# A fused attention and FFN kernel on one core: transposes of head pairs give way to x's, statistics are released after the second block-product group, and kept products run on ScalarE or VectorE

## The chip, the core and the metric

One core of a Trainium2 chip runs the whole program. Its engines are TensorE (PE in the profile; PEld is its weight load), VectorE (DVE), ScalarE (ACT), GpSimd (POOL) and SyncE (SP, which only issues DMAs). ScalarE and GpSimd issue DMAs too. Each engine works through its own instructions strictly in order; what is still waiting at the head of a queue holds up everything behind it. The metric is the device time of the program in microseconds, as the median of several runs.

## The reference

```python
# q, k, v: 8 batches, 12 heads, 448 positions, 64 wide
scores = scale * np.matmul(q, k.transpose(0, 1, 3, 2))
attn = np.maximum(scores, 0.0) ** 2 / S
attn_out = np.matmul(attn, v)
x = attn_out.transpose(0, 2, 1, 3).reshape(B, S, H * D)      # 8 x 448 x 768
mu, var = mean and variance of x over its 768 columns
xn = (x - mu) / np.sqrt(var + 1e-06) * g_ln
ch = np.maximum(xn @ w_ch1, 0.0) @ w_ch2                     # 768 -> 3072 -> 768
return x + ch
```

The output is float32. The kernel computes in bfloat16 with float32 sums. It leaves the division by the standard deviation to the end: the factor `rstd` of a row passes through the ReLU and is applied when the second FFN product is evacuated.

## The kernel before, in words

**Stages.** The eight batches `b` follow each other. While the FFN of one batch runs on TensorE, the attention of the next is slipped in between in "visits". Attention works on three pairs of head groups per batch, numbered `n` = 3b to 3b+2 (`NPER` = 3). A pair's q and k come in by GpSimd DMAs into one staging tile (`load_pair`, L423), are turned by one SyncE DMA transpose (L429) into one of two slots (`RING` = 2), and are used by seven score products (`att_QK`, L610). Each score tile is scaled and clipped by ScalarE (L619) or VectorE (L621) and squared by VectorE (L634) or, rarely, by GpSimd (L636). `att_AV` (L676) multiplies by v into a PSUM tile, which is copied in two parts to `xT_all` (L385 on ScalarE, L387 on VectorE): 2x384 columns and 2x64 columns. GpSimd sums these parts for the mean (L767 to L770). `after_x` turns x back with SyncE DMA transposes into `x_all` (L797), takes batch statistics from there on VectorE (`bn_stats` L822 and L825, `bn_aggr` L828), the root on ScalarE (L838) and the reciprocal on VectorE (L840). The result is `rstd`.

**First FFN product.** `ffn_1` (L971) and `ffn_1_slot` (L989) make one 128-row tile of hidden units with six matmuls. For batches 3 to 6, three groups (`G_STEADY` = 3) of four tiles are instead made with seven block products, P1 to P7, instead of eight (`ffn_1_product`, L1193; a Strassen-like scheme). In each group the two PSUM banks are reused, so three intermediate results are copied out and kept: c1 after P1, c2 after P6, p5 after P5 (`keep`, L1225). `add_relu` (L1219) adds a kept result to a bank and applies ReLU on VectorE: C11 after P2, C22 after P7, C12 after P3. C21 is a plain ReLU after P4 (L1234). The group's three banks of work depend on each other: P6 needs c1 out, P5 needs C11 out, P7 needs c2 out, P3 needs p5 out, P4 needs C22 out. The kept tiles lie in `o_all`, whose two rows also carry finished output to the store DMAs, so a keep waits for the last store of that row (`o_done`).

**Second FFN product.** `ffn_w` (L1428) does the same with pairs of 128-row output tiles, again in seven products; its evacuations (L1436) multiply by `rstd` and add x. `ffn_2` (L1519, evacuated by L1535) is the plain form. `store_tile` (L1557) sends the results out from ScalarE's and SyncE's queues. L1384 and L1066 to L1070 are VectorE's block sums for the two schemes.

**What sets the order.** Nothing runs by the order of the source. `Order` is a planner: each piece of work is an `Op` with candidate engines, a cost in ns for each, dependencies, and a `key` (lower goes first among equals). `best` takes the op that can start first by the planner's clock, and for an op with several engines the engine that would finish it first; `commit` emits the instruction then and there and advances that engine's clock. `segment` chooses at each step between the FFN's next product and the next attention visit by the same clock. So a dependency or a cost that is written into the planner changes in which order, and on which engine, everything afterwards is emitted; the waits that the hardware sees come from the data alone. `later(...)` is a dependency on something not yet planned and `now_known` fills it in. `stats_gate` is such a dependency: for batches 3 to 6 the statistics (keyed 4.0 down to 3.8, after almost everything) may be planned only once `"seven past"` is filled in, which happens when the last of the three groups is through. In `commit`, a DMA on SyncE occupies that engine's clock for 0.55 of its modelled transfer.

Of the kernel before, what the change touches and what calls it, by code (L numbers as in the profile page):

```python
# [41 lines left out]
class Order:  # L42
# [39 lines left out]
    def commit(self, op, eng, t0):  # L82
        cost = op.cost[op.engs.index(eng)] if isinstance(op.cost, tuple) else op.cost
        if op.load is not None and eng != "POOL":
            t0 = max(t0, self.lanes[-8])
        op.t0 = t0
        self.free[eng] = t0 + cost - (self.OVER[eng] if op.load is None else 0.0)
        if op.port and eng in self.port:
            self.port[eng] = t0 + cost - (140.0 if eng == "POOL" else 0.0)
        if op.load is not None and eng == "POOL":  # L90
            total, each = op.load
            start = max(self.dma_free, t0 + cost + 1300.0)
            self.dma_free = start + total
            self.loads.append((start, self.dma_free, each))
            op.t1 = self.dma_free + 700.0
        elif op.load is not None:
            left, each = op.load
            start = t = max(self.ring[eng], t0 + cost + 1300.0)
            while left > 0:
                edge, wait = None, 0.0  # L100
                for a, z, e in self.loads:
                    if a <= t < z:
                        edge, wait = z, e
                    elif t < a and (edge is None or a < edge) and not wait:
                        edge = a
                rate = 16.0 / (each + wait)
                span = left / rate if edge is None else min(left / rate, edge - t)
                left -= rate * span
                t += span
                if left < 1e-6:  # L110
                    break
            self.ring[eng] = t
            self.lanes.append(t + 900.0)
            if eng == "SP":
                self.free["SP"] = t0 + max(cost, 0.55 * (t - start))
            op.t1 = t + 900.0 + (0.2 * (t - start) if eng == "SP" else 0.0)
        else:
            op.t1 = t0 + cost + self.LAT[eng]
        op.emit(eng)
        self.log.append((t0, cost, eng, op))  # L120
# [82 lines left out]
def kernel(  # L203
# [10 lines left out]
    nc = tc.nc  # L214
# [3 lines left out]
    Act = mybir.ActivationFunctionType  # L218
# [195 lines left out]
    def load_pair(n):  # L414

        b, pn = divmod(n, NPER)
        free = [ops["qk_free", 0]] if n == 2 * NPER else [later("turn", n - 1)]
        ld = []
        for t, src in enumerate((q, k)):
            for half in range(2):  # L420
                def emit(eng, t=t, src=src, half=half):
                    h0 = half * 6 + 2 * pn
                    nc.gpsimd.dma_start(  # L423
                        qk_stage()[half * T:(half + 1) * T, t].rearrange("p j (h d) -> p j h d", d=D),
                        src[b, h0:h0 + 2].rearrange("h (p j) d -> p j h d", j=J))
                ld.append(load(dma_ns(2 * S, 256), emit, free, 900.0))

        def turn(eng):
            nc.sync.dma_start_transpose(qk_slot(n).rearrange("p t j c -> p (t j) c"),  # L429
                                        qk_stage().rearrange("p t j c -> p (t j c)"))  # L430
        free = [later("qk_end", n - RING)] if n >= 2 * NPER + RING else []
        ops["turn", n] = R.add("SP", 100.0, turn, ld + free, key=0.0, load=(2 * J * P, 18.0))
        now_known(ops["turn", n], "turn", n)
        ld = []
        free = [later("av_end", n - RING)] if n >= 2 * NPER + RING else [later("av_done", 1)]
        for half in range(2):
            def emit(eng, half=half):
                if "v" not in homes:
                    v_t = v_pool.tile([P, H // 2 * S], bf16, tag="v1")
                    homes["v"] = v_t  # L440
                h0 = half * 6 + 2 * pn
                nc.gpsimd.dma_start(  # L442
                    v_slot(n)[half * T:(half + 1) * T],
                    v[b, h0:h0 + 2].rearrange("h (p j) d -> p h (j d)", j=J))
            ld.append(load(dma_ns(2 * T, 1792), emit, free, 700.0))
        ops["v_ld", n] = ld
# [213 lines left out]
    def att_AV(n, s):  # L660
# [28 lines left out]
        if b == 0:  # L689
            for half in range(2):  # L690
                def evac(eng, half=half):
                    ki = pn + half * NPER
                    copy(eng, xT_of(b)[:, ki, :], av_st[n][half])
                ev = R.add(("DVE", "ACT"), (620.0, 560.0), evac, [op], key=-1.0)
                f_use(ev)
                evs.append(ev)
        else:
            def evac(eng, cols, o):
                i = av_st[n, 1][:, :, cols]
                if len(o.shape) == 4:  # L700
                    o, i = o.rearrange("p m h c -> p h m c"), i.rearrange("p h (m c) -> p h m c", c=P)
                copy(eng, o, i)
            if b == 1:
                parts = [(slice(0, S), xT_of(b)[:, pn::NPER, :])]
            else:
                t, t_left = xT_of(b)
                parts = [(reg(b), t[:, :, pn::NPER, :]), (left(b), t_left[:, pn::NPER, :])]
            for cols, o in parts:
                w = cols.stop - cols.start
                evs.append(R.add(("DVE", "ACT"), (160.0 + 2.08 * w, 150.0 + 1.7 * w),  # L710
                                 lambda eng, cols=cols, o=o: evac(eng, cols, o), [op] + free, key=-1.0))
            slot_use(evs)
        ops["x", n] = evs
        if n == NPER - 1:
            for ev in held_relu:
# [401 lines left out]
    W_OF = {"P1": ("A", 0, 0), "P2": ("A", 0, 1), "P6": "S2", "P5": "S1", "P7": "S3", "P3": "S4", "P4": ("A", 1, 1)}  # L1117
    X_OF = {"P1": "B11", "P2": "B21", "P6": "T2", "P5": "T1", "P7": "T3", "P3": "B22", "P4": "T4"}

    FLIGHT = 4  # L1120
    AWAY = 1700.0

# [47 lines left out]
    def ffn_1_product(b, g, name):  # L1170
# [51 lines left out]

        def keep(key):
            def emit(eng):
                nc.scalar.copy(kept(key), e["ps", bank])  # L1225
            free = [later("av_done", b)] if b == LAST_B else o_done[e["o"] if key == "c2" else 1 - e["o"]]
            e[key] = R.add("ACT", 560.0, emit, [op, *free], key=-3.0)
        if name in ("P1", "P6", "P5"):
            keep({"P1": "c1", "P6": "c2", "P5": "p5"}[name])
        elif name != "P4":  # L1230
            add_relu(*{"P2": ("C11", 0, 0, "c1"), "P7": ("C22", 1, 1, "p5"), "P3": ("C12", 0, 1, "c2")}[name])
        else:
            def relu(eng):
                nc.scalar.activation(h_out(1, 0), e["ps", "x"], Act.Relu)  # L1234
            e["C21"] = R.add("ACT", 560.0, relu, [op], key=-3.0)
            if b < LAST_B:
                f_banks[:] = [e["C12"], e["C21"]]
                f_tags.reverse()
# [3 lines left out]
            h_done(b, range(4 * g, 4 * g + 4), [e[c] for c in ("C11", "C12", "C21", "C22")], op)  # L1242
            if b < LAST_B and g == G_STEADY - 1:
                now_known(op, "x sums used", b)
                now_known(e["C12"], "seven past", b, 5)
                now_known(e["C21"], "seven past", b, 15)

# [615 lines left out]
```

## Time and profile before

| what | value |
|---|---|
| median of 3 runs | 527.24 us (527.17 to 527.32) |
| the profiled execution's own time | 527.36 us |
| its span, first to last instruction | 525.6 us |
| granted TensorE clock | 1.000 |
| TensorE busy | 503.0 us, 4416 matmuls |
| VectorE busy | 390.8 us, 738 instructions |
| ScalarE busy | 236.9 us, 373 instructions |
| GpSimd busy | 170.4 us, 201 instructions |
| score ReLU on ScalarE, L619 | 127 x 927 ns |
| score ReLU on VectorE, L621 | 32 x 1087 ns |
| squares on VectorE, L634 | 158 x 720 ns |
| x's DMA transposes, L797 | 21, median 8.0 us from issue to landing |
| pairs' DMA transposes, L429 | 18, median 4.4 us from issue to landing |
| keeps in `o_all` on ScalarE, L1225 | 36 x 535 ns |

The span is what the instructions fill; the run's own time is 1.76 us longer. In the listing of a timeline, a line has its start and length in us, the engine, the source line, output and input tiles, the shape and the number of merged instructions; a bracket at the end tells how long the engine stood idle before it and which instruction ended that wait. Busy time adds the records of an engine; a sum over windows shows where an engine is idle.

### The profile page before, as it was taken

To read this page: it belongs to the slowest core of one execution; us is meant where nothing else is said; L and a number is where in the kernel's file an instruction comes from. 1 tells how busy PE (TensorE), PEld (TensorE's weight loads), DVE (VectorE), ACT (ScalarE), POOL (GpSimd) and SP (SyncE) were. 2 spreads that over 40 slices of the span, in tenths; PEclk is the share of its full clock that TensorE was granted. 3 is DMA by queue.
4 is the path that set the end of the run, shared out by engine and by line. 5 is a ranking of instruction groups with operands and counts; after the bars stand their busy time and mean duration, and the time that the engine had idled before them with its cause. 6 is when DMAs were issued, how large, how long until landed. Compare 5 with 4: busy or idle time off the path is not lost.

```text
span 525.6 us, 10787 instructions
## 1 busy us (share of the span) xinstructions
PE 503.0 (96%) x4416; PEld 305.8 (58%) x4416; DVE 390.8 (74%) x738; ACT 236.9 (45%) x373; POOL 170.4 (32%) x201
## 2 busy tenths in 40 slices
PE   4899999999999999999899999999999999999997
PEld 3444455455564445567456675566655666569864
DVE  5988648946887878855988479756789578976853
ACT  5977612523214654255622676145722466125300
POOL 7420501434542545451650455323633022200000
PEclk9999999999999999999999999999999999999999
DMA  9999999889777848892992976966883610123022
GB/s 190 197 186 195 199 193 127 80 107 137 82 143 81 80 64 102 106 152 36 90 109 54 126 77 81 114 110 56 89 99 65 126 19 2 30 58 64 2 62 60
DMA packets 145949, 51.89 MB, mean 99 GB/s; under 512 B 123238, under 2 KB 144108, under 8 KB 145900
## 3 DMA queue, kind: packets, MB, share of 16 engines
q0 software_dynamic: 82224, 25.50, 45.8%
q1 hardware_dynamic: 59036, 18.82, 20.8%
q10 hardware_dynamic: 4640, 6.88, 4.6%
q8 instruction: 34, 0.56, 0.4%
q14 instruction: 15, 0.12, 0.1%
HBM read 51.91 MB, written 11.01 MB: 120 GB/s over the span
## 4 chain that ended last, share of the span: by engine, by line
PE 76%; DVE 10%; DMA 4%; ACT 4%; issue 3%; POOL 2%; SPq 0%; ACTq 0%; DVEq 0%; POOLq 0%
PE f_ps L1428 20%; PE f_ps L971 16%; PE f_ps L1519 12%; PE f_ps L1193 8%; PE ps L989 5%; PE sc L610 5%; PE ps L676 4%; DVE at_all L634 4%; PE x_ps L1193 2%; DMA out_dram<-o_all 2%; ACT at_all L619 2%; PE y_ps L1193 2%; ACT xT_all L385 1%; DMA x_all<-xT_all 1%; DMA f<-in_k_dram 1%
## 5 line engine op out<-in xcount | busy, mean ns | idle before, releaser
L619 ACT ACTIVATE at_all<-sc 128x896 bf16<-128x896 f32 x127 | 110.6, 927 | 74.0 <-PE sc L610 67.9
L634 DVE TENSOR_TENSOR at_all<-at_all 128x896 bf16<-128x896 bf16 x158 | 110.0, 720 | 1.3 <-ACT at_all L619 1.2
L1428 PEld LDWEIGHTS <-h 128*128 128x128 bf16 x708 | 68.5, 98 | 50.5 <-issue 6.3
L971 PE MATMUL f_ps<-a,w 128*128 128x448 bf16 x474 | 93.6, 353 | 0.2 <-DVE h L1002 0.2
L423 POOL DMA_DIRECT2D t<-in_q_dram x36 | 41.9, 1314 | 133.8 <-DMA t<-t 112.6
L971 PEld LDWEIGHTS <-w 128*128 128x128 bf16 x474 | 44.9, 98 | 45.3 <-issue 5.8
L1428 PE MATMUL f_ps<-w,h 128*128 128x384 bf16 x360 | 62.8, 326 | 1.6 <-DVE o_all L1436 1.0
L442 POOL DMA_DIRECT2D v_t<-in_v_dram x36 | 27.2, 820 | 93.3 <-PE sc L610 66.5
L423 POOL DMA_DIRECT2D t<-in_k_dram x36 | 55.0, 2083 | 0.0
L610 PE MATMUL sc<-t 64*64 64x448 bf16 x672 | 49.3, 364 | 3.8 <-ACT at_all L619 2.0
L621 DVE TENSOR_SCALAR at_all<-sc 128x896 bf16<-128x896 f32 x32 | 34.8, 1087 | 22.8 <-PE ps L676 18.6
L1000 ACT ACTIVATE h<-f_ps 128x448 bf16<-128x448 f32 (+1 forms) x59 | 29.3, 497 | 43.8 <-PE f_ps L971 42.2
L989 PE MATMUL ps<-a,w 128*128 128x448 bf16 x228 | 48.3, 352 | 0.8 <-DVE xT_all L387 0.8
L1193 PEld LDWEIGHTS <-w 128*128 128x128 bf16 x432 | 40.7, 98 | 8.9 <-issue 6.7
L1219 DVE CUSTOM_DVE_ANT_0 h<-f_ps,o_all 128x448 bf16<-128x448 f32 x36 | 21.8, 618 | 29.0 <-ACT h L1000 21.2
L1519 PE MATMUL f_ps<-w,h 128*128 128x384 bf16 x240 | 40.2, 326 | 0.0
L610 PEld LDWEIGHTS <-t 64*64 64x64 bf16 x672 | 18.3, 106 | 26.7 <-issue 18.6
L1193 PEld LDWEIGHTS <-t 128*128 128x128 bf16 x318 | 30.3, 98 | 5.6 <-issue 2.3
L769 POOL TENSOR_TENSOR sum_t<-sum_t,xT_all 128x384 f32<-128x384 f32 (+2 forms) x25 | 23.4, 935 | 31.1 <-ACT xT_all L385 30.8
L1519 PEld LDWEIGHTS <-h 128*128 128x128 bf16 x240 | 23.2, 98 | 16.5 <-issue 1.4
L989 PEld LDWEIGHTS <-w 128*128 128x128 bf16 x228 | 22.2, 98 | 15.9 <-issue 0.9
L1000 ACT ACTIVATE h<-ps 128x448 bf16<-128x448 f32 x39 | 20.8, 545 | 21.9 <-PE ps L989 21.6
(152 smaller groups left out, 720.1 us busy)
## 6 DMA issues: line engine op xcount, KB each, us to landing
w<-in_moe_w_ch_dram POOLq DMA_DIRECT2D x4, 1152.0 KB, 38.5
out_dram<-o_all ACTq DMA_DIRECT2D x43, 96.0 KB, 2.4
t<-in_q_dram POOLq DMA_DIRECT2D x36, 112.0 KB, 4.3
t<-in_k_dram POOLq DMA_DIRECT2D x36, 112.0 KB, 5.2
v_t<-in_v_dram POOLq DMA_DIRECT2D x36, 112.0 KB, 3.4
out_dram<-o_all SPq DMA_DIRECT2D x35, 96.0 KB, 2.1
w<-in_moe_w_ch_dram POOLq DMA_DIRECT2D x4, 768.0 KB, 20.0
out_dram<-o_all ACTq DMA_DIRECT2D x13, 192.0 KB, 3.9
```

Of the source, the lines that this page charges most:

```text
L423: nc.gpsimd.dma_start(qk_stage()[half * T:(half + 1) * T, t].rearrange("p j (h d) -> p j h d", d=D), src[b, h0:h0 + 2].rearrange("h (p j) ...
L442: nc.gpsimd.dma_start(v_slot(n)[half * T:(half + 1) * T], v[b, h0:h0 + 2].rearrange("h (p j) d -> p h (j d)", j=J))
L610: nc.tensor.matmul(sc[rows_of(half), r, :S], turned[rows_of(r), 1, s, rows_of(half)], turned[rows_of(r), 0, :, rows_of(half)], start=True, ...
L619: nc.scalar.activation(attn[n, s], st[0][:, :, :S], Act.Relu, scale=rc2)
L621: nc.vector.tensor_scalar(attn[n, s], st[0][:, :, :S], rc2, 0.0, op0=Alu.mult, op1=Alu.max)
L634: nc.vector.tensor_mul(attn[n, s], attn[n, s], attn[n, s])
L971: nc.tensor.matmul(st[0], w1[:, ki, ni * P:(ni + 1) * P], xc[b][:, ki, :], start=(i == 0), stop=(i == K1 - 1))
L989: nc.tensor.matmul(st[0], w1[:, ki, ni * P:(ni + 1) * P], xc[b][:, ki, :], start=ki == 0, stop=ki == K1 - 1)
L1000: nc.scalar.activation(o, st[0][:, c], Act.Relu)
L1193: nc.tensor.matmul(e["ps", bank][:, n, :], a[:, k, n * P:(n + 1) * P], x[:, k, :], start=name in ("P1", "P2", "P5") and n == 0 and k == 0, ...
L1428: nc.tensor.matmul(e["ps", bank], a(k), w(k), start=new and k == 0, stop=k == KH - 1, skip_group_check=True)
L1519: nc.tensor.matmul(o_st["ps"], stat(u, m, ki), w2[:, ki, j * hd:(j + 1) * hd], start=(ki == 0), stop=(ki == K2 - 1))
```

## The change

Six edits. In the planner, a SyncE DMA whose descriptor cost is under 20 (the DMA transposes, which carry 18.0) occupies SyncE's clock for 1.3 instead of 0.55 of its modelled transfer. A pair's transpose may be planned only after the whole AV product of the pair two before it, and not merely after that pair's score products. The second part of an AV evacuation is planned after the first, and the PSUM slot is free after the last part. A kept product and the ReLU after P4 may go to ScalarE (560) or VectorE (620). The statistics' two gates are filled in after the second of three groups. No matmul is added or removed.

```diff
             if eng == "SP":
-                self.free["SP"] = t0 + max(cost, 0.55 * (t - start))
+                self.free["SP"] = t0 + max(cost, (1.3 if op.load[1] < 20.0 else 0.55) * (t - start))
...
-        free = [later("qk_end", n - RING)] if n >= 2 * NPER + RING else []
+        free = [later("qk_end", n - RING), later("av_end", n - RING)] if n >= 2 * NPER + RING else []
         ops["turn", n] = R.add("SP", 100.0, turn, ld + free, key=0.0, load=(2 * J * P, 18.0))
...
                 evs.append(R.add(("DVE", "ACT"), (160.0 + 2.08 * w, 150.0 + 1.7 * w),
-                                 lambda eng, cols=cols, o=o: evac(eng, cols, o), [op] + free, key=-1.0))
-            slot_use(evs)
+                                 lambda eng, cols=cols, o=o: evac(eng, cols, o), [op] + free + evs, key=-1.0))
+            slot_use(evs[-1])
...
+    EITHER = (("ACT", "DVE"), (560.0, 620.0))
...
         def keep(key):
             def emit(eng):
-                nc.scalar.copy(kept(key), e["ps", bank])
+                copy(eng, kept(key), e["ps", bank])
             free = [later("av_done", b)] if b == LAST_B else o_done[e["o"] if key == "c2" else 1 - e["o"]]
-            e[key] = R.add("ACT", 560.0, emit, [op, *free], key=-3.0)
+            e[key] = R.add(*EITHER, emit, [op, *free], key=-3.0)
...
             def relu(eng):
-                nc.scalar.activation(h_out(1, 0), e["ps", "x"], Act.Relu)
-            e["C21"] = R.add("ACT", 560.0, relu, [op], key=-3.0)
+                if eng == "ACT":
+                    nc.scalar.activation(h_out(1, 0), e["ps", "x"], Act.Relu)
+                else:
+                    nc.vector.tensor_scalar(h_out(1, 0), e["ps", "x"], 0.0, None, op0=Alu.max)
+            e["C21"] = R.add(*EITHER, relu, [op], key=-3.0)
...
             if b < LAST_B and g == G_STEADY - 1:
                 now_known(op, "x sums used", b)
+            if b < LAST_B and g == 1:
                 now_known(e["C12"], "seven past", b, 5)
                 now_known(e["C21"], "seven past", b, 15)
```

## The prediction, made before the changed kernel was run

> **What bounds the kernel now.** I read the page's busy times first, then the windows, then TensorE's timeline for every wait, then the other engines around the longest ones.
>
> ```profile
> PE 503.0 (96%) x4416; PEld 305.8 (58%) x4416; DVE 390.8 (74%) x738; ACT 236.9 (45%) x373; POOL 170.4 (32%) x201
> PEclk9999999999999999999999999999999999999999
> ```
>
> ```profile
> 30.00:180.00 150.00, 150.00 (x1220) 78.92 (x1219) 110.67 (x226) 66.30 (x108) 50.54 (x55) 1.00 0.96 134
> 180.00:462.00 282.00, 272.69 (x2307) 168.38 (x2305) 218.59 (x392) 134.44 (x210) 104.04 (x121) 1.00 0.65 82
> ```
>
> TensorE bounds it, at full clock. From 30 to 180 us its records leave no idle time; from 180 to 462 us, where batches 3 to 6 run, they leave 282.00 - 272.69 = 9.3 us. The matmuls are not touched, so an order that removed every wait there would gain 9.3 us. That caps the change. These are the longer waits:
>
> ```profile
> 195.24 0.97 PE L1428 MATMUL f_ps<-w,h 128*128 128x384 bf16 x5 [0.57 <-DVE h L1002]
> 234.11 1.30 PE L989 MATMUL ps<-a,w 128*128 128x448 bf16 x6 [0.77 <-DVE xT_all L387]
> 260.54 0.32 PE L1428 MATMUL f_ps<-v_t,x_all 128*128 128x384 bf16 x1 [1.15 <-DVE o_all L1436]
> 295.00 0.73 PE L1193 MATMUL f_ps<-t,w 128*128 128x224 bf16 x6 [0.52 <-ACT o_all L1225]
> 331.62 1.14 PE L1428 MATMUL f_ps<-v_t,h 128*128 128x384 bf16 x6 [0.48 <-DVE o_all L1436]
> 365.53 0.73 PE L1193 MATMUL f_ps<-v_t,w 128*128 128x224 bf16 x6 [1.11 <-DVE h L1219]
> 385.63 0.32 PE L1428 MATMUL f_ps<-v_t,x_all 128*128 128x384 bf16 x1 [1.20 <-DVE o_all L1436]
> 428.45 0.74 PE L1193 MATMUL f_ps<-x_all,t 128*128 128x224 bf16 x6 [0.71 <-DVE h L1219]
> 458.31 2.11 PE L1428 MATMUL f_ps<-w,h 128*128 128x384 bf16 x12 [0.99 <-DVE o_all L1436]
> ```
>
> They add to 7.50 us; the other 1.8 us are waits under 0.25 us. Nearly all were ended by VectorE. Around 260 us it did this:
>
> ```profile
> 254.30 1.00 DVE L822 BATCH_NORM_STATS2 st<-x_all 128x6 f32<-128x384 bf16 x2
> 255.23 0.99 DVE L825 BATCH_NORM_STATS2 st<-x_all 128x6 f32<-128x384 bf16 x2
> 259.27 0.17 DVE L840 RECIPROCAL r_t<-r_t 128x4 f32<-128x4 f32 x1
> 259.87 0.61 DVE L1436 SCALAR_TENSOR_TENSOR o_all<-f_ps,r_t,x_all 128x384 f32<-128x384 f32 x1
> 362.12 1.82 DVE L634 TENSOR_TENSOR at_all<-at_all 128x896 bf16<-128x896 bf16 x1
> 363.86 1.08 DVE L621 TENSOR_SCALAR at_all<-sc 128x896 bf16<-128x896 f32 x1
> ```
>
> The first evacuation of the second product (259.87) stood behind statistics that were still running. At 362 a different thing: one square took 1.82 us and then a ReLU came before the L1219 that TensorE needed.
>
> **The change, part by part.** What goes where I take from the changed program's order of instructions, which holds no times.
>
> *Statistics gate.* In batches 3 and 5 the reciprocal now stands before the last P1/P2 of the second product begin: two attention visits and four first-product tiles lie between. The 1.15 and 1.20 us waits end: -2.35 us. If other work slides into the place, 0.
>
> *Evacuations in batches 4 and 6.* The wait at 331.62 came from four squares (3.65 us) in front of an L1436, the one at 458.31 from two pairs of w1 sums (1.16 + 1.26 us). In the new order L1436 stands ahead of the squares, and one pair of sums is behind it: -1.4 of 1.47 us; at worst 0.
>
> *Keeps and ReLU on either engine.* In batches 4 and 6, after the first AV of the period, c2 and p5 move to VectorE and stand before the squares; the L1219 that follows has a product and a score visit (0.58 + 0.69 us) more in front of its user: -(1.11 + 0.71). The same reordering puts the ReLU before 195.24 on ScalarE, which has it done 0.2 us before its user: -0.57. Sum -2.4; at worst 0, since the order may be late elsewhere.
>
> *SyncE's order.* Here is batch 3 before:
>
> ```profile
> 221.55 2.55 SPq L429 DMA_TRANSPOSE t<-t  x1
> 224.19 1.04 SPq L1557 DMA_DIRECT2D out_dram<-o_all  x1
> 225.35 3.38 SPq L797 DMA_TRANSPOSE x_all<-xT_all  x1
> ```
>
> A pair's transpose was issued before a store and before x's transpose; that landed 7.50 us after its issue (chain of waits), 232.85, and the copy into `xT_all` that must not overwrite what it reads waited for it; TensorE lost 0.77. Now store, x, pair: x's transpose is issued near 222.6 and lands near 230.1. The copy would be ready at about 229.0, so some wait stays on VectorE, where the copy now is and where a square and an L1219 queue behind it: I take -0.4 (0 to -0.77). At the start of batch 4 the store also escapes the pair's transpose, and the 0.52 us wait of a keep for it goes: -0.5.
> The pair's transpose comes 4 to 8 us later, and GpSimd's loads of the next pair wait for its landing (112.6 us of waits already), as do stores queued behind it on SyncE. What covers that: after each pair transpose in batches 3 to 6 at least some 12 us of matmuls stand before its first user, against 4.4 us to land. I cost it at 0; uncovered, it would be the lateness itself, up to 4 us per pair.
>
> *The second evacuation part.* Before, VectorE took it in 17 of 18 cases and stood idle 10.2 us in all for ScalarE's part. Now nine go to ScalarE, behind the first part. That frees VectorE but is not on TensorE's path; 0, apart from the terms above.
>
> *What is added.* VectorE gets 7 more L621 (7 x 1.087), 8 keeps (0.615, as L387's 128x448), 2 ReLUs after P4 and 5 on L989's tiles (7 x 0.617), one more large copy (0.957) and about 0.8 of ReLU parts; it loses 8 small copies (0.292) and 4 squares (0.615). Sum 7.6 + 4.9 + 4.3 + 1.0 + 0.8 - 2.3 - 2.5 = +13.8 us, 74% to 77% busy. It is hidden under TensorE where an evacuation has a product or more in front of its user. Seven hidden tiles go from L989 to L971 at the same matmul pitch: 0. In batches 3 and 5 the p5/c2 keeps come sooner after a 192 KB store (3.9 us to land) because fewer L989 tiles stand between: +0.3 (0 to +0.8).
> Four squares go to GpSimd, which has none in the trace. Nearest rows: its 384-column add, 1.13 us, as a floor, and that times 896/384 = 2.6 us as a ceiling; I take 2.6, the same kind of work by size. Two stand in a row in batch 3 with about 7 us of products before their AV: hidden. But VectorE's squares that overlap GpSimd's adds have a median of 1.23 us against 0.615, so up to 1.2 us may be lost by each of the four: +0.2, range 0 to +2.
>
> The Trainium skill, SBUF page, "Practical consequences": a VectorE instruction with two SBUF inputs and a GpSimd instruction that reads SBUF exclude each other, the loser blocked for the other's whole length. It speaks against the four squares: by it a two-input VectorE instruction behind each could stand 2.6 us, together 10.4 us if all reached TensorE, and the sum would be a slower kernel. The trace agrees in kind: statistics and L1219, with fewer SBUF inputs, keep their length under GpSimd's adds, and it is these that stand beside the four.
>
> *New waits I can't see.* A new order makes new near misses. For these I take +2.0 us, a little more than the 1.8 us of small waits that the old order has, from 0 to +5.
>
> Sum: -2.35 - 1.4 - 2.4 - 0.4 - 0.5 + 0.3 + 0.2 + 2.0 = -4.55 us. Span 525.6 - 4.55 = 521.05; with the 1.76 us around the span 522.8; the profiled run is 0.12 above the median, so 522.7 us.
>
> **The rivals.** *Half is given back (chance 0.22).* The gate and store terms hold (-2.35 - 0.5), the others return as new waits of VectorE with its 13.8 us more: 527.24 - 2.85 + about 2 = 526.4, from 525.5 to 527.5. For it: VectorE is 78% busy from 180 to 462 us (218.59 / 282.00). Against: the order puts evacuations ahead of squares.
>
> *VectorE becomes the late engine in the third group (chance 0.14): slower.* The statistics (per batch four times 0.54 + 0.54 + 0.20 = 5.1 us) now lie among the third group's block products, where C11, C22 and C12 gate TensorE. Cover is one product (0.58) for C11, a product and a tile (0.58 + 1.14 = 1.7 us) for C22. If all three come one 0.54 us statistic beyond their cover in each of four batches, that is 12 x 0.54 = 6.5 us; with only -2.85 of the gains, 527.24 + 3.65 = 530.9. It decides once VectorE's queue in front of a C22 is over 1.7 us. For it: statistics and two ReLUs stand between these L1219s. Against: I count about 1.2 us in front of the worst one.
>
> *The change does not do what it says (0.04).* Statistics planned earlier wait for x's transposes, at the head of VectorE's queue. Against: they are issued 10 us of products before. 527.2.
>
> **How the numbers follow.** The forecast case has 0.60: 522.7, by its own terms 519.8 to 525.5. The half case adds the middle. Two in ten lie outside 520.0 to 528.0. What this kernel's measurement can tell from no change is 0.2%, 1.05 us. Faster: 0.60 + half of 0.22 + a little = 0.72; same: the rest of the half case and the empty case, 0.13; slower 0.15.
>
> **What would show it.** Right: TensorE's idle time from 180 to 462 us falls from 9.3 to near 5; the waits for L1436 at the first P6 of batches 3 and 5 are gone; x's transpose follows its store directly on SyncE. Wrong: waits of L1193 for L1219 in the third group, long L634 beside L636, or waits of L610 for a pair's transpose.

## The result, and the profile after

The changed kernel takes 518.35 us (median of 4 runs, 517.86 to 519.64) against 527.28 us (527.17 to 527.42) for the kernel before on the same chip: a ratio of 0.9834, 95% interval 0.9815 to 0.9853, so 8.9 us less. The profiled run took 518.0 us; its span is 516.1 us, 9.5 us shorter. The forecast was 522.7 us, in 520.0 to 528.0: the direction was right, the gain nearly twice the forecast one.

The busy times and the granted clock on the page of the changed kernel:

```profile
PE 500.2 (97%) x4416; PEld 305.8 (59%) x4416; DVE 397.5 (77%) x751; ACT 225.4 (44%) x356; POOL 178.3 (35%) x205
PEclk9999999999999999999999999999999999999999
```

The same two windows as before (start and end, length, then busy time and instructions of TensorE, its weight loads, VectorE, ScalarE and GpSimd, granted clock, DMA share, GB/s):

```profile
30.00:180.00 150.00, 148.80 (x1204) 78.03 (x1206) 113.60 (x229) 61.79 (x102) 46.73 (x50) 1.00 0.96 133
180.00:462.00 282.00, 280.36 (x2391) 175.17 (x2384) 228.88 (x416) 128.76 (x202) 115.41 (x128) 1.00 0.67 84
```

Idle time from 180 to 462 us fell from 9.3 to 1.6 us; in the window before it, 1.2 us are new. TensorE's timeline has these waits over 0.15 us left behind 30 us:

```profile
161.09 0.35 PE L971 MATMUL f_ps<-a,w 128*128 128x448 bf16 x1 [0.26 <-DVE a L891]
161.61 1.29 PE L971 MATMUL f_ps<-a,w 128*128 128x448 bf16 x6 [0.17 <-DVE o_all L1441]
163.67 2.62 PE L971 MATMUL f_ps<-a,w 128*128 128x448 bf16 x13 [0.77 <-DVE h L1002]
226.63 0.73 PE L1194 MATMUL f_ps<-t,w 128*128 128x224 bf16 x6 [0.87 <-DVE o_all L387]
347.31 0.73 PE L1194 MATMUL f_ps<-t,w 128*128 128x224 bf16 x6 [0.62 <-ACT o_all L385]
```

None of the nine named waits is among them. They are new: three behind VectorE near 161 us, two for a keep.

**How much TensorE stood still.** Here is the first surprise: the span shrank by 9.5 us, more than the 9.3 us that were to cap the change, and TensorE's busy time went down by 2.8 us with the same 4416 matmuls. The record of a 448-column matmul is 0.353 us long, but the next one usually starts 0.189 us later. So the first 0.16 us of every wait are covered by the record in front of it, and a wait shorter than that leaves no idle time at all. Measured from start to start (each distance less the usual one of that pair of lines, counted over 0.1 us), the stall from 180 to 462 us was 12.9 us before and is 2.1 us now, from 140 to 180 us it rose from 0 to 1.7, and in the whole span it fell from 21.8 to 12.4: 9.4 us, which is the 9.5 us of the span. "Stall" below means this.

**VectorE and SyncE.** The statistics' reciprocal now stands 8 us in front of the first evacuation that needs it, and that evacuation waited for TensorE, not the other way round. The page's group of squares is shorter: before it was 158 of 720 ns.

```profile
247.86 0.18 DVE L840 RECIPROCAL r_t<-r_t 128x4 f32<-128x4 f32 x1 [0.36 <-ACT r_t L838]
255.78 0.62 DVE L1441 SCALAR_TENSOR_TENSOR o_all<-f_ps,r_t,x_all 128x384 f32<-128x384 f32 x1 [0.75 <-PE f_ps L1433]
```

```profile
L634 DVE TENSOR_TENSOR at_all<-at_all 128x896 bf16<-128x896 bf16 x154 | 96.8, 660 | 1.9 <-ACT at_all L619 1.9
```

On SyncE, x's transpose follows the store and the pair's comes last, as the new order said:

```profile
214.13 7.41 SPq L1562 DMA_DIRECT2D out_dram<-o_all  x2
221.63 5.13 SPq L797 DMA_TRANSPOSE x_all<-xT_all  x1
227.87 1.53 SPq L429 DMA_TRANSPOSE t<-t  x1
```

**What the squares show.** A square of 128x896 takes 0.615 us when nothing is in its way. Adding up what each L634 took beyond that gives 17.1 us in the kernel before (14 squares above 1.29 us) and 7.3 us now (6 of them, the longest 1.45). The 1.82 us square at 362.12 that the prediction showed was one of these. GpSimd did this beside it:

```profile
361.32 1.19 POOL L442 DMA_DIRECT2D v_t<-in_v_dram  x2 [4.51 <-PE sc L610]
362.51 1.59 POOL L767 TENSOR_TENSOR sum_t<-xT_all 128x384 f32<-128x384 bf16 x2
```

VectorE had just finished the small part of an AV evacuation (0.29 us, at 361.92), which is what GpSimd's sums wait for. Its next instruction was the square. The two ran into each other, and the ReLU, the L1219 and TensorE's 1.11 us wait stood behind. Its squares of 1.5 us or more stand at 193, 208, 270, 362, 378, 395.6 and 426 us, and within 3 us behind six of them (all but 378) a TensorE wait follows. That made the edit to the evacuation, costed at nothing, a suspect.

### The profile page after: what moved, and what is told of

Same layout as the page of the kernel before. It is cut to its first block, busy times and chain, and to the rows that moved or that the text cites. A ratio compares the mean times of both kernels' runs of the same rounds, so it can differ in the third digit from the quotient of the medians.

```text
span 516.1 us, 10774 instructions
## 1 busy us (share of the span) xinstructions
PE 500.2 (97%) x4416; PEld 305.8 (59%) x4416; DVE 397.5 (77%) x751; ACT 225.4 (44%) x356; POOL 178.3 (35%) x205
## 4 chain that ended last, share of the span: by engine, by line
PE 91%; DVE 5%; DMA 2%; ACT 1%; issue 1%; DVEq 0%; ACTq 0%
PE f_ps L1433 25%; PE f_ps L971 19%; PE f_ps L1524 12%; PE f_ps L1194 10%; PE sc L610 7%; PE ps L989 6%; PE ps L676 6%; PE x_ps L1194 2%; PE y_ps L1194 2%; DVE at_all L634 1%; DMA out_dram<-o_all 1%; DVE t L387 1%; DMA f<-in_q_dram 1%; DVE a L891 1%; ACT at_all L619 1%
## 5 line engine op out<-in xcount | busy, mean ns | idle before, releaser
L619 ACT ACTIVATE at_all<-sc 128x896 bf16<-128x896 f32 x120 | 105.4, 924 | 78.8 <-PE sc L610 75.8
L971 PE MATMUL f_ps<-a,w 128*128 128x448 bf16 x516 | 102.0, 353 | 1.2 <-DVE h L1002 0.8
L634 DVE TENSOR_TENSOR at_all<-at_all 128x896 bf16<-128x896 bf16 x154 | 96.8, 660 | 1.9 <-ACT at_all L619 1.9
L442 POOL DMA_DIRECT2D v_t<-in_v_dram x36 | 21.5, 604 | 168.1 <-PE sc L610 147.5
L971 PEld LDWEIGHTS <-w 128*128 128x128 bf16 x516 | 48.9, 98 | 50.5 <-issue 7.5
L423 POOL DMA_DIRECT2D t<-in_k_dram x36 | 55.9, 2132 | 0.0
L423 POOL DMA_DIRECT2D t<-in_q_dram x36 | 42.1, 1344 | 38.1 <-DMA t<-t 26.7
L621 DVE TENSOR_SCALAR at_all<-sc 128x896 bf16<-128x896 f32 x39 | 42.4, 1088 | 15.7 <-PE ps L676 8.7
L1194 PEld LDWEIGHTS <-w 128*128 128x128 bf16 x432 | 41.0, 98 | 7.7 <-issue 4.7
L989 PE MATMUL ps<-a,w 128*128 128x448 bf16 x186 | 40.2, 352 | 0.0
L1220 DVE CUSTOM_DVE_ANT_0 h<-f_ps,o_all 128x448 bf16<-128x448 f32 x36 | 21.8, 619 | 21.3 <-PE f_ps L1194 12.6
L1194 PEld LDWEIGHTS <-t 128*128 128x128 bf16 x318 | 30.2, 98 | 4.1 <-issue 1.3
L1441 DVE SCALAR_TENSOR_TENSOR o_all<-f_ps,r_t,x_all 128x384 f32<-128x384 f32 x39 | 23.9, 613 | 11.0 <-PE f_ps L1433 10.8
L385 ACT CAST xT_all<-ps 128x768 bf16<-128x768 f32 (+2 forms) x28 | 17.8, 641 | 28.7 <-PE ps L676 17.7
L676 PE MATMUL ps<-at_all,v_t 64*64 64x448 bf16 x552 | 29.8, 350 | 0.0
```

The costliest lines, as they stand in the source:

```text
L423: nc.gpsimd.dma_start(qk_stage()[half * T:(half + 1) * T, t].rearrange("p j (h d) -> p j h d", d=D), src[b, h0:h0 + 2].rearrange("h (p j) ...
L619: nc.scalar.activation(attn[n, s], st[0][:, :, :S], Act.Relu, scale=rc2)
L621: nc.vector.tensor_scalar(attn[n, s], st[0][:, :, :S], rc2, 0.0, op0=Alu.mult, op1=Alu.max)
L634: nc.vector.tensor_mul(attn[n, s], attn[n, s], attn[n, s])
L676: nc.tensor.matmul(av_st[n][half][rows_of(hh)], (v_slot(n)[rows_of(half), hh] if b > 1 else vt[b][rows_of(half), 2 * pn + hh])[:, s * D:(s ...
L971: nc.tensor.matmul(st[0], w1[:, ki, ni * P:(ni + 1) * P], xc[b][:, ki, :], start=(i == 0), stop=(i == K1 - 1))
```

## The experiments

Expectations speak of three theories at first: 1, each edit is worth the waits that the prediction gave it; 2, the order as a whole (or SyncE's) counts; 3, redundant edits. Times are medians of 4 runs or more, the ratio is to the kernel before on the same chip (527.1 to 527.6 us). Stall is that from 140 to 462 us in the profiled run; "squares lost" is what L634 took beyond 0.615 us each, whole span. Both are of one run each, which need not be the median one: for the kernel with the chain undone it is the longest of six, 535.28 us, and some 3 of its us are two spells of half clock (last section).

| kernel | us | ratio, 95% | stall | squares lost |
|---|---|---|---|---|
| before | 527.28 | | 12.9 | 17.1 |
| changed | 518.35 | 0.9834 (0.9815 to 0.9853) | 3.8 | 7.3 |
| changed, gate undone | 519.35 | 0.9843 (0.9815 to 0.9872) | 5.6 | 5.0 |
| changed, keeps and ReLU undone | 518.30 | 0.9823 (0.9790 to 0.9855) | 3.2 | 7.9 |
| changed, SyncE's cost undone | 518.49 | 0.9828 (0.9797 to 0.9859) | 3.2 | 7.6 |
| changed, pair's wait for the AV undone | 520.75 | 0.9878 (0.9846 to 0.9909) | 5.5 | 6.9 |
| changed, chain of the evacuation undone | 531.83 | 1.0077 (1.0045 to 1.0108) | 18.7 | 21.5 |
| before + pair's wait alone | 524.38 | 0.9946 (0.9924 to 0.9967) | 9.7 | 17.9 |
| before + gate alone | 525.99 | 0.9978 (0.9964 to 0.9992) | 12.1 | 19.4 |
| before + keeps and ReLU alone | 527.60 | 1.0002 (0.9989 to 1.0015) | 13.1 | 17.8 |
| before + chain alone | 521.45 | 0.9894 (0.9879 to 0.9908) | 7.4 | 5.7 |
| before + chain and pair's wait | 518.22 | 0.9819 (0.9803 to 0.9835) | 2.9 | 5.7 |
| chain undone, sums cut | 519.98 | 0.9863 (0.9846 to 0.9879) | 6.3 | 3.0 |
| before, sums cut | 518.04 | 0.9835 (0.9817 to 0.9853) | 4.2 | 3.0 |
| chain undone, small part on ScalarE | 520.00 | 0.9860 (0.9844 to 0.9876) | 5.4 | 5.7 |
| chain undone, sums only write | 518.66 | 0.9830 (0.9812 to 0.9847) | 4.6 | 2.9 |
| changed, sums cut | 518.35 | 0.9824 (0.9806 to 0.9841) | 3.9 | 2.5 |
| changed, two gains to ScalarE | 517.74 | 0.9809 (0.9793 to 0.9826) | 2.6 | 7.2 |
| changed, run again | 519.11 | 0.9837 (0.9815 to 0.9860) | 6.4 | 7.2 |
| two gains to ScalarE, run again | 517.63 | 0.9803 (0.9787 to 0.9820) | 5.7 | 7.4 |

### One edit undone

Statistics released by the third group:

```diff
             if b < LAST_B and g == G_STEADY - 1:
                 now_known(op, "x sums used", b)
-            if b < LAST_B and g == 1:
                 now_known(e["C12"], "seven past", b, 5)
                 now_known(e["C21"], "seven past", b, 15)
```

> The changed kernel with one edit undone: the statistics are released after the third group again. Theory 1 (each edit is worth the waits that the prediction gave to it): the two waits of the first L1441 of the second product come back, 1.15 + 1.20 us of idle time and about 0.16 us more each that the record of the last matmul covers, so +2.7 us on 518.35: 521.0. Theory 2 (the gain belongs to the order as a whole, and each undone edit shuffles all later waits): a stall from 140 to 462 us between 6 and 13 us instead of 3.8, so 520.5 to 527.5, with most waits in other places than the two named. Theory 3, on the cap: against the changed kernel the span moves by the difference of the start-to-start excess of the matmuls within 0.3 us, and the idle time in the records shows about 0.16 us less for each wait.

519.35 us, 1.0 over the changed kernel, which the spread of the runs does not clear (518.72 to 519.98 against 517.86 to 519.64). Neither wait at the first evacuation came back; its stalls sit at the keeps (1.68 us at 227, 1.03 at 349). The statistics run late again there, but the order has one more first-product tile in front of that evacuation, so the cover is there anyway. Theories 1 and 2 both miss. Between the two profiled runs the span moved by 2.1 us and the stall of the whole span by 2.1, as theory 3 of the expectation said.

Keeps and ReLU on ScalarE alone (`copy(eng, ...)` and both `EITHER` taken back):

> The changed kernel with kept products and the ReLU after P4 on ScalarE alone again. Theory 1: the waits of L1194 for a L1220 that stands behind squares come back (1.11 + 0.71 us) and the one of 0.57 us, with 0.16 us each on top: +2.9 us, 521.2. Theory 2: 520.5 to 527.5, the waits elsewhere. A rival: keeps on VectorE were not needed and cost VectorE 9 us of work; then it is 517 to 518.4 and the two keep waits of the changed kernel (1.04 and 0.79 us) are gone.

518.30 us: no difference that can be told. The waits at 365 and 428 us did not return. The time is the rival's, its sign only in part: one keep wait is nearly gone (0.16 us at 227.6), the other stays (0.90 at 348). The edit did not earn what it was given.

SyncE's clock:

```diff
-                self.free["SP"] = t0 + max(cost, (1.3 if op.load[1] < 20.0 else 0.55) * (t - start))
+                self.free["SP"] = t0 + max(cost, 0.55 * (t - start))
```

> The changed kernel with the planner's occupancy of SyncE by a transpose back at 0.55 instead of 1.3. Theory 1: a pair's transpose comes before x's again, the copy into xT_all waits (0.77 + 0.16 us) and the store before the keep is late (0.52 + 0.16): +1.6 us, 520.0; by the prediction's own terms +0.9. Theory 2: 520.5 to 527.5.

518.49 us: no difference that can be told, against both theories, and x's transpose still follows the store at once. So this cost is not what orders SyncE.

The pair's transpose released by the scores alone:

```diff
-        free = [later("qk_end", n - RING), later("av_end", n - RING)] if ...
+        free = [later("qk_end", n - RING)] if n >= 2 * NPER + RING else []
```

> The changed kernel with a pair's transpose released by the score products alone, as before. Theory 1 (costed at 0): 518.0 to 518.8, with the later pair transposes back at their old places in the queue and nothing on TensorE's path changed. Theory 2: 520.5 to 527.5 although no wait was assigned to this edit.

520.75 us, 2.4 more, and SyncE is back at the order of the kernel before (pair's transpose at 223.8, store, x's at 227.4). This edit is the one that lets x's transposes go first. The two profiled spans differ by 2.8 us: 1.7 us is more stall from 140 to 462 us, and about 1 lies in the first 30 us, where nothing was changed. The largest wait that the changed kernel does not have is TensorE's for GpSimd's sums:

```profile
216.89 0.35 PE L861 MATMUL slot<-rsum_t,ones 128*128 128x448 bf16 x1 [0.74 <-POOL rsum_t L770]
```

GpSimd issued the next pair's loads (L423) at 210.29 and 214.98, in front of the sums and between them; in the changed kernel, where the pair's transpose comes later, the loads start at 217.32, behind the last sum, and TensorE does not wait there.

The chain of the evacuation:

```diff
-                                 ..., [op] + free + evs, key=-1.0))
-            slot_use(evs[-1])
+                                 ..., [op] + free, key=-1.0))
+            slot_use(evs)
```

> The changed kernel with the two parts of an AV evacuation planned side by side again. TensorE's and SyncE's orders are those of the changed kernel; 22 more instructions' worth of evacuations go to VectorE. The prediction costed this edit at 0: 518.0 to 518.8. A rival: the ScalarE parts behind the first part are what keeps VectorE free for L1220 and L1441; then VectorE's waits come back and it is 520 to 523.

531.83 us: 13.5 us lost, slower than the kernel before and far outside both expectations, with TensorE's and SyncE's orders those of the changed kernel. 18 squares took more than 1.29 us. (VectorE has 4 instructions more than in the changed kernel, 755 against 751, and not the 22 of the expectation.) One place, VectorE's timeline, then GpSimd's, then TensorE's (a bracket: idle before, and what ended it):

```profile
320.22 0.29 DVE L387 CAST xT_all<-ps 128x128 bf16<-128x128 f32 x1 [0.43 <-ACT xT_all L385]
320.42 3.11 DVE L634 TENSOR_TENSOR at_all<-at_all 128x896 bf16<-128x896 bf16 x2
323.46 0.61 DVE L1002 TENSOR_SCALAR h<-f_ps 128x448 bf16<-128x448 f32 x1
```

```profile
319.61 1.24 POOL L442 DMA_DIRECT2D v_t<-in_v_dram  x2 [5.58 <-PE sc L610]
320.85 0.94 POOL L769 TENSOR_TENSOR sum_t<-sum_t,xT_all 128x384 f32<-128x384 f32 x1
321.87 1.18 POOL L770 TENSOR_TENSOR sum_t<-sum_t,xT_all 128x384 f32<-128x384 f32 x1
```

```profile
324.12 4.12 PE L971 MATMUL f_ps<-a,w 128*128 128x448 bf16 x12 [2.00 <-DVE h L1002]
```

The small part on VectorE ends, GpSimd's sums start, and the two squares behind it take 3.11 instead of 1.16 us. The ReLU L1002, which TensorE needs, is 1.95 us late, and TensorE idles 2.00 us.

### Alone on the kernel before, and the sums taken away

> The kernel before with one edit alone: a pair's transpose waits for the whole AV product two pairs earlier. Of the four single undos only this one cost 2 us or more (520.75), and with the gate undone neither wait at the first P6 came back. Theory 1 (the prediction's terms, this edit at 0): 527.3. Theory 2 (the order of SyncE is what counts, and this edit carries it: x's transposes and stores move ahead of the pair's, batch statistics and keeps come in time): at least half of the gain alone, 520 to 523, start-to-start stall from 180 to 462 us under 7 us against 13.0 before. Theory 3 (redundant edits: any two of them give the whole gain): 520 to 525 for every single edit.

524.38 us, -2.9 alone. Theory 2's half of the gain was not reached, theory 1's zero is wrong. The waits for x's transpose (0.94 at 234), for the store (0.68 at 295) and most of those at the first evacuations (1.31 to 0.29, 1.37 to none) went; the squares' loss stayed at 17.9 us. So this gain is not the squares'.

> The kernel before with the statistics released by the second group alone. Theory 1: the two waits of the first L1436 of batches 3 and 5 go (1.31 + 1.37 us start to start), 524.6. Theory 2: little, 526 to 527.5, since x's transpose still stands behind the pair's on SyncE. Theory 3: 520 to 525.

525.99 us, -1.3: half of what theory 1 gave it. The two waits went; new or longer ones (0.57 at 274 and 398 us, 0.74 instead of 0.34 at 316) took part of it back.

> The kernel before with the kept products and the ReLU after P4 on ScalarE or VectorE alone. Theory 1: the waits of L1193 at 365.5 and 428.5 us and the one at 195.2 go (1.27 + 0.88 + 0.73 us), 524.4. Theory 2: 526 to 528. Theory 3: 520 to 525.

527.60 us: nothing, although the sum had 2.4 us for it.

> The kernel before with one edit alone: the second part of an AV evacuation behind the first. New theory (the clash): when VectorE takes the small part, its next instruction is a square, and the small part is just what releases GpSimd's sums; a square that runs beside them takes 1.3 to 1.8 us instead of 0.615, and the L1219 or L1436 behind it is late. In the kernel before, the squares lost 17.1 us in this way, and nine TensorE waits end within 4 us after one of 1.3 us or more (0.73 + 0.22 + 0.38 + 0.19 + 0.65 + 1.27 + 0.24 + 0.21 + 0.88 = 4.8 us start to start). With the part on ScalarE the sums start later, beside other work: 527.3 - 4.8 = 522.5, and the squares' loss falls below 9 us. Theory 1 (costed at 0): 527.3.

521.45 us, -5.7 alone, the largest of all; the squares' loss fell to 5.7 us as foretold. The sum of the two larger single gains is 8.6 us.

To see whether it is really the sums, they were cut in the kernel with the chain undone, with every order kept:

```diff
...
+                x0, x1, s0, r_t = ((a[:, :, :4] if len(a.shape) == 3 else a[:, :4]) if b >= 3 else a for a in (x0, x1, s0, r_t))
```

> The kernel with the chaining undone (531.8), its order of instructions on TensorE, VectorE, ScalarE and SyncE kept exactly, and from batch 3 on GpSimd's sums cut to 4 columns a piece: most of the sum over the columns is left out, so the means are not those of the reference. The clash theory: no long squares from batch 3 on (21.5 us lost before, then under 4 in all), the two waits of 1.9 and 2.0 us with the half clock behind them go, 518 to 521. Rival (22 more evacuations on VectorE and PSUM freed later make it late by themselves): the waits stay, 528 to 532.

519.98 us, 11.9 less than with the sums. The same place, VectorE's timeline and GpSimd's:

```profile
314.19 0.29 DVE L387 CAST xT_all<-ps 128x128 bf16<-128x128 f32 x1 [0.43 <-ACT xT_all L385]
314.40 1.16 DVE L634 TENSOR_TENSOR at_all<-at_all 128x896 bf16<-128x896 bf16 x2
```

```profile
313.58 1.25 POOL L442 DMA_DIRECT2D v_t<-in_v_dram  x2 [5.40 <-PE sc L610]
314.82 0.25 POOL L769 TENSOR_TENSOR sum_t<-sum_t,xT_all 128x12 f32<-128x12 f32 x1
```

Same instructions in the same order, and the two squares take 1.16 us. GpSimd's load issues (L442) are still there, so they are not what blocks. One of the two long waits stayed (2.01 us at 228): that one is a keep behind a store.

> The kernel before with the same cut of GpSimd's sums from batch 3 on (most of the sum is left out), all orders kept. The clash theory: the waits that follow a long square in batches 3 to 6 go, 4.8 us at most, so 522.5 to 524; the waits for statistics (1.31 + 1.37 us), for the stores and for x's transpose stay. Rival (the squares' length is hidden, the order is what counts): 526.5 to 527.5.

518.04 us: the kernel before, with not one of the six edits, is as fast as the changed one once the sums are gone. The expectation of 522.5 was too small, because it counted only the waits right behind a long square. TensorE's window from 180 to 462 us, with the columns as above:

```profile
180.00:462.00 282.00, 279.17 (x2370) 173.55 (x2363) 210.96 (x407) 136.13 (x212) 83.26 (x122) 1.00 0.66 83
```

VectorE has 7.6 us less work in it than in the kernel before (218.59), and stall is down from 12.9 to 4.2 us; of the waits at the first evacuations (1.31 and 1.37 us) 0.43 each is left. What looked like late statistics was mostly VectorE late from its squares. The waits for x's transpose and for the store stay, as expected (0.93 us idle at 233.67, 0.53 at 293.18). They are the ones that the pair's wait removes, so these 9 us are not made of the same pieces as the change's 9 us.

> The kernel with the chaining undone, but with the small part of every AV evacuation on ScalarE, planned beside the large one. The clash theory in its form that the engine counts (VectorE does not release the sums in front of its own square): 518 to 521. In its form that the delay by the chain counts: the sums start as early as without the chain, long squares stay, 525 to 532.

520.00 us: with the small part on ScalarE, and no chain, the squares' loss is 5.7 us. So it is the engine that counts. The chain works because it makes the planner choose ScalarE for nine of these parts. (One wait of 1.79 us, at 228, is part of the time here.)

### What blocks, what is left, and what suffices

In the next kernel GpSimd's sums were replaced by small adds that keep their waits, and by fills of the whole piece:

```diff
+                fill = (lambda o: [nc.gpsimd.memset(o, 0.25) for _ in range(2)]) if b >= 3 else (lambda o: None)
...
+                    nc.gpsimd.tensor_add(s0, x0, x1); fill(o0)
...
```

> The kernel with the chaining undone; from batch 3 on each of GpSimd's sums is replaced by an add of 4 columns, which keeps its wait, and two fills of the whole piece, which only write. The sums are left out, so the means are not the reference's; the orders on the other engines are kept. Theory A (what blocks a square is GpSimd reading on-chip memory): squares from batch 3 on stay at 0.615 us, 518.6 to 521. Theory B (any GpSimd instruction that moves data blocks it): squares of 1.2 us and more stay where the fills run, 525 to 533.

518.66 us. GpSimd is as busy as with the sums (183.5 against 180.4 us), VectorE is down from 410.6 to 389.4 us. VectorE's timeline at the same place, then GpSimd's:

```profile
313.00 1.16 DVE L634 TENSOR_TENSOR at_all<-at_all 128x896 bf16<-128x896 bf16 x2
314.08 0.61 DVE L1005 TENSOR_SCALAR h<-f_ps 128x448 bf16<-128x448 f32 x1
```

```profile
313.42 0.25 POOL L772 TENSOR_TENSOR sum_t<-sum_t,xT_all 128x12 f32<-128x12 f32 x1
313.73 0.89 POOL L765 MEMSET sum_t<- 128x384 f32 x2
314.70 0.59 POOL L773 TENSOR_TENSOR sum_t<-sum_t,xT_all 128x12 f32<-128x12 f32 x1
```

Fills beside a square cost it next to nothing (27 squares ran beside fills, none took over 0.644 us); adds that read cost it up to 1.2 us. The Trainium skill, page "SBUF — State Buffer", section "Practical consequences", says this: a VectorE instruction with two SBUF inputs contends with a GpSimd instruction that reads SBUF, and not with one that only writes. These two runs agree, and the prediction had cited the rule, but held it only against the four squares that moved.

> The changed kernel with GpSimd's sums cut to 4 columns from batch 3 on (most of the sum is left out), all orders kept. If what is left of the clash (squares that lose 7.3 us, of which about 4 us from batch 3 on) still reaches TensorE: 516 to 517.5. If it is hidden, as the changed kernel's waits suggest (none of the six that are left follows a long square): 518 to 518.7.

518.35 us, the changed kernel's time to the digit. What is left of the clash from batch 3 on is hidden there.

The waits near 161 us are new. In the changed kernel VectorE had four gains (L891) in a row while GpSimd issued a pair's loads; VectorE's and GpSimd's timelines:

```profile
157.89 3.14 DVE L891 TENSOR_SCALAR a<-a,g_sb 128x448 bf16<-128x448 bf16 x4
```

```profile
157.41 2.35 POOL L423 DMA_DIRECT2D t<-in_q_dram  x2 [6.98 <-DMA t<-t]
159.06 3.05 POOL L423 DMA_DIRECT2D t<-in_k_dram  x2
```

Alone, a gain takes 0.34 us; here the four took 0.78, 1.32, 0.32 and 0.96.

```diff
-                c_ops.append(R.add(*GAIN_ON, lambda eng, ki=ki: gain(eng, ki), subs, ...
+                c_ops.append(R.add(GAIN_ON[0], (665.0, 335.0 if b != 2 else 700.0), lambda eng, ki=ki: gain(eng, ki), subs, ...
```

> The changed kernel, and in batch 2 two of the five gains (L891) go from VectorE to ScalarE; TensorE's, GpSimd's and SyncE's orders are kept. In the changed kernel four of them took 3.14 us instead of 4 x 0.34 while GpSimd issued loads (L423), and the three waits right behind (0.42 + 0.33 + 0.93 us) are new against the kernel before. Theory: a second clash, of VectorE's two-byte scalar operations with GpSimd's issuing; VectorE is through some 1.3 to 1.7 us sooner and most of the 1.7 us goes: 516.7 to 517.4. Rival: the two on ScalarE end as late, 518 to 519.

517.74 us, between the two expectations; the stall near 161 us fell from 1.68 to 0.27 us, though one of the two gains left still took 1.32. (That GpSimd's issuing is what lengthens a gain was not tested by itself: two gains fewer also leave VectorE less work.)

```profile
157.90 1.59 DVE L891 TENSOR_SCALAR a<-a,g_sb 128x448 bf16<-128x448 bf16 x2
```

Four runs each do not tell it from the changed kernel. Both ran once more, side by side on one chip:

> The changed kernel once more, beside the one with batch 2's two gains on ScalarE on the same chip, since 517.74 and 518.35 lay closer than the spread of four runs each: 518.0 to 518.8.

> The changed kernel with two of batch 2's gains on ScalarE once more. If the 1.4 us of stall that its trace lacks near 161 us are a gain in time: 0.6 to 1.4 us under the changed kernel of this call. If they are given back later: within 0.3 us of it.

519.11 us (518.20 to 520.73) for the changed kernel and 517.63 us (517.26 to 520.13, 6 runs) with the two gains moved; ratios 0.9837 (0.9815 to 0.9860) and 0.9803 (0.9787 to 0.9820). The first is over its range of 518.0 to 518.8, and the 1.5 us between them are a little more than the 0.6 to 1.4 foretold. Over both sets of runs the medians are 518.68 (8 runs) and 517.63 (10 runs). The kernel with two gains moved is likely the fastest of this study, by about 1 us; the intervals still overlap.

> The kernel before with two edits alone: the pair's transpose behind the AV product (alone 524.4) and the chained evacuation (alone 521.45). If these two carry the change: 518 to 519.3, the sum of both alone being -2.9 - 5.7 = -8.6 us. If the other three edits matter beside them: 520 to 521.5.

518.22 us. Two of the six edits make the whole change; the gate, the keeps and the ReLU, and SyncE's cost add nothing that can be told beside them. The chain's share is the squares' (loss 17.1 to 5.7 us); the pair's wait leaves them alone and takes away the waits for x's transpose, the store and GpSimd's sums.

## Why the forecast was too small, step by step

**The step that failed** is "The second evacuation part ... That frees VectorE but is not on TensorE's path; 0". It is the largest term: -5.7 us alone, 13.5 us when it is taken out of the changed kernel. Mis-sized beside it is SyncE's order, -0.9 in the sum: the edit that carries it, the pair's wait for the AV, is worth -2.9 us alone and 2.4 us when taken out. The prediction saw the pieces (squares with a median of 1.23 us beside GpSimd's adds, the 1.82 us square in front of a late L1219) and used them only for the four squares that go to GpSimd. It did not ask which instruction releases those adds. That is the small part itself, so the engine that does it decides what the adds run into. The kernel before with the sums cut shows that without the clash, and what it delays, that kernel too is 9 us faster. (Cutting them also shortens GpSimd's work; that this does not matter was shown with the fills for the kernel with the chain undone, and was not tried on the kernel before.) Two of the prediction's three signs of being right came (the waits at the first P6 gone, x's transpose behind its store) and the third overshot (1.6 us idle, not 5); none of them tells the named edits from the clash.

**The cap** of 9.3 us was wrong as an argument: idle time in the records leaves out 0.16 us of every wait. The stall there was 12.9 us, and the order removed 10.8 of it.

**The evacuations in batches 4 and 6 (-1.4) and the keeps and ReLU (-2.4).** The waits they name are gone, but not by these edits: keeps alone give 0, undoing them costs 0, and with nothing but the sums cut from the kernel before none of these five waits is there. The prices were right for the waits and booked to the wrong cause; that the waits went all the same is luck.

**The gate (-2.35).** Its two waits are gone, but they were over-determined: gate alone -1.3, gate undone +1.0 (within the spread) with the waits still absent, and cutting the sums alone brings them from 1.31 and 1.37 to 0.43 each.

**SyncE's order (-0.9).** The mechanism was right (waits of 0.94 and 0.68 us start to start are gone), the carrier was not the SyncE cost but the pair's wait for the AV, and that edit was worth more, -2.9 alone. With it alone x's transposes land sooner (230.05 against 232.86 us in batch 3, 352.10 against 358.13 in batch 5), and the waits at the first evacuations shrink; that they shrink because the statistics come sooner is argued, not tested. The lateness of the pair's transposes, costed at 0, showed no wait for a pair's transpose in TensorE's list.

**Keeps sooner after a store (+0.3).** Right in kind, too small: 1.04 and 0.79 us start to start at 226.6 and 347.3, a sum of 1.8 where the upper bound was 0.8. The first keep waited 1.25 us for the store to land, and the second started 0.15 us after its store had landed (346.58).

**Four squares on GpSimd (+0.2).** They took 1.68 us each, between the floor of 1.13 and the ceiling of 2.6, and the statistics and L1220 beside them kept their 0.54 and 0.61 us: 0.

**VectorE's added work.** +13.8 us was forecast, +6.7 measured (390.8 to 397.5): the squares gave 9.8 us back, the slow gains took 3.2 (8.7 to 11.9).

**Unseen waits (+2.0).** New stall is 1.7 us near 161 and 2.1 behind it, 3.8 in all; but the small waits that were taken to stay, 12.9 - 9.0 = 3.9 us start to start, went too. The forecast was -7.05 for the named waits and +2.5 for all that is added, -4.55. Measured in stall: -9.0 for the nine named waits, -3.9 for the small ones, +3.8 new, and -0.3 in the first 30 us: -9.4. The slower rival did not come up: no L1194 waited behind statistics in a third group.

Still open: how much of the 2.4 us with the pair's wait undone is the first 30 us, whose stall differs from run to run (7.9 to 9.5 us over all profiles), and why it differs.

## What to carry to other kernels

Before costing a small copy that changes engine, look up what it releases: here a copy on VectorE that released GpSimd's adds started them just beside VectorE's own next instruction. Where one form of instruction has two lengths in a trace, list what ran beside the long ones before reading the waits behind them; cutting the suspected neighbour's work with all orders kept is an experiment of one line. And take TensorE's stall from start to start of its matmuls: idle time between its records is short by the pipelined part of each wait.

## What the runs showed of the hardware

**Reading blocks, writing does not**: 100 fills on GpSimd with 28.4 us in all left every square beside them at 0.61 to 0.64 us, and adds of the same pieces stretched them to 1.3 to 1.86 us. Gains with one bfloat16 input went from 0.34 to as much as 1.32 us beside GpSimd's load issuing, where squares with two inputs kept their length beside L442's issuing (in the runs with the sums cut).

**A long wait costs the clock too.** In the second profile of the changed kernel the keep's wait at 226 us was 2.13 instead of 0.87 us (a store landed later), and the matmuls behind it ran at half pace; TensorE's timeline, then a window with the granted clock, 0.57, in the third column from the right:

```profile
227.75 0.73 PE L1194 MATMUL f_ps<-t,w 128*128 128x224 bf16 x6 [2.13 <-DVE o_all L387]
```

```profile
229.00:232.50 3.50, 3.50 (x42) 1.66 (x44) 2.70 (x5) 0.92 (x1) 0.00 (x0) 0.57 0.71 136
```

The slow starts last about 3.5 us and cost some 1.5 us; that profile's run took 520.73 us, the first one's 518.0. The second profile of the kernel with two gains moved has the same spell behind a wait of 2.06 us, in a run of 520.13 us. The kernel with the chain undone has two such spells, behind waits of 1.88 and 2.00 us (starts 0.37 us apart instead of 0.19 from 324.1 to 327.6). A wait of 2.01 us in the kernel with the chain undone and the sums cut had none, nor had any of 1.63 us or less. So waits near 2 us are where it may happen. The changed kernel's runs spread over 2.9 us (517.86 to 520.73); the wait for the store and its spell account for the two that were profiled, and for the others this is not shown.
